# Attention and two MoE layers on one core: first-pass scores on 128 rows, scores cut at 512 columns, and constant matmuls in planned pauses

## Chip, cores and metric

One core of one Trainium2 chip. The metric is device time of one execution in microseconds (us), smaller is better; the time before is the median of three runs. Engines are named as the profile names them: PE (TensorE matmul), PEld (TensorE weight load), DVE (VectorE), ACT (ScalarE), POOL (GpSimd), SP (SyncE, which issues all DMAs here).

## What is computed

Batch 4, 8 heads, 576 positions, head size 64; then two MoE-like layers on 2304 tokens with 512 features and 2048 hidden units.

```
scores = q @ k.T / 8
attn   = exp(scores - max), kept only where scores >= max - tau, divided by its sum
x      = attn @ v                       # rearranged to [2304, 512]
x      = (h * clip(h + 3, 0, 6) / 6) @ w_out,     h = x @ w_in
out    = (h * sigmoid(1.702 * h)) @ w2_out,       h = x @ w2_in
```

## The kernel before

The kernel writes every operation into a list (`add`, line 300) with an engine, a cost in ns, a nominal time and its reads and writes. `Plan.settle` (line 220) runs a list scheduler over that list with those costs, and the operations are issued in the order of the planned starts (line 1075). So a cost written in the code sets the order in which instructions stand on each engine; it does not change how long they take.

Attention works in 16 units, a unit being a batch and a pair of heads (`unit`, line 486). A unit has nine score tiles of 128 queries by 576 keys. Each tile goes through the same chain: scores on PE into PSUM (`ps`, a ring of two places), row maximum on DVE (R, line 589), threshold (TH, line 590), exponential on ACT (X, line 591), mask and sum on DVE (M, line 592). Then `e` is transposed (line 643 and `blocks`) and multiplied with v (lines 684 and 701). The ring of two means that the scores of a tile can start only when M of the tile two before it is done.

Units 0 to 3 (batch 0, `early`) take the scores in plain fp32 (`score`, line 564) in two passes: pass 0 covers the first 256 queries of both heads, four tiles, each alone; pass 1 the rest, in pairs of heads. The two heads of a unit lie on rows 0 to 63 and 64 to 127 of one tile of q and one of k, and a single-head tile uses the 64 rows of its head. The trace shows an fp32 matmul as two records. Units 4 to 15 (`score2`, line 550) take them in fp32r: the keys are split in a high part `kh` and a low part `kl`, and a score tile is four matmuls, high and low times the two halves of the keys, 288 columns each (the fifth tile has eight). Each of them loads its 128 x 128 weights anew. I call four such matmuls a set.

Beside the attention of batch 0, 16 weight tiles of the first layer are decoded from 64-bit words (`decode`, line 376: ACT lines 347 and 400, DVE lines 401 to 403, POOL line 350) and split (`split`, line 407). The layer's matmuls (`gated`, line 750, line 760; `out_mm`, line 777, line 780) run between the score tiles of the next batch, in PSUM tiles `pm` of four banks.

`two` (line 368) is a constant of zeros and ones, set by three memsets on POOL. `g` is a ring of eight buffers for the hidden activations.

Of the kernel before, what the change touches and what calls it, by code (L numbers as in the profile page):

```python
# [9 lines left out]
F32 = mybir.dt.float32  # L10
F32R = mybir.dt.float32r
# [7 lines left out]
P = 128  # L19
# [41 lines left out]
class Plan:  # L61
# [158 lines left out]
    def settle(self):  # L220
# [9 lines left out]
            length = self.order(key)  # L230
        return sorted(self.ops, key=lambda o: (self.start[o.n], o.n))


def kicked(key, length, seed):

# [7 lines left out]
def tile_top_attention_moe_moe2(  # L243
# [19 lines left out]
    HF = NF // 2  # L263
    SH = S // 2
    CH = [(0, 256), (256, 320)]
    FULL = EXACT = 4
    scale = 0.125


# [58 lines left out]
    def f32(ap):  # L328
        return ap.bitcast(F32)

    def pe(n):
        return 7 + 0.43 * n
# [152 lines left out]

    def unit(u, b, j, t0):

        early, exact = u < FULL, u < EXACT
# [8 lines left out]
        def tile_():  # L497
            return buf("kqv", 12, "st", [P, QC], F32R)

        if exact:  # L500
            khb, qhb = tile_(), tile_()
        pieces = [(0, 0, 0, S)] + ([(1, 0, 0, 256), (1, 256, 320, 256), (1, 576, 256, 64)] if b == 0 else [(1, 0, 64, 512), (1, 576, 0, 64)])

        def of_head(x, hd):
            return [(x, ("z", hd))] + [(x, (h, o)) for h, o, _, _ in pieces if h == hd]

        def load_q(x, ap):
            for hd, z in ((0, 576), (1, 512)):
                add(POOL, 100, K("ld"), "qz", lambda hd=hd, z=z: nc.gpsimd.memset(ap()[64 * hd:64 * hd + 64, z:z + 64], 0.0), [], [(x, ("z", hd))])
            for hd, o, i, n in pieces:  # L510
                move(K("ld"), "ldq", 256 * n, lambda hd=hd, o=o, i=i, n=n: nc.sync.dma_start(out=ap()[64 * hd:64 * hd + 64, o:o + n], in_=q2[b, 2 * j + hd, :64, i:i + n]), [], [(x, (hd, o))])

        def load_k(x, ap):
            for hd in range(2):
                move(K("ld"), "ldk", 256 * S, lambda hd=hd: nc.sync.dma_start(out=ap()[64 * hd:64 * hd + 64, :S], in_=k2[b, 2 * j + hd, :64]), [], [(x, hd)])

        if exact:
            load_q(qhb, lambda: f32(qhb.t))
            load_k(khb, lambda: f32(khb.t))
            for rows, hds in ((slice(0, 64), (0,)), (slice(64, P), (1,))) if u == 0 else ((slice(0, P), (0, 1)),):  # L520
                add(DVE, 69 + 0.521 * QC, K("qs"), "qs", lambda rows=rows: nc.vector.tensor_scalar(out=f32(qhb.t)[rows], in0=f32(qhb.t)[rows], scalar1=sc_b.t[rows], scalar2=1.0, op0=ALU.mult, op1=ALU.mult),
                    [sc_b], [x for hd in hds for x in of_head(qhb, hd)])
# [26 lines left out]

        def score2(s):  # L550

            ps, t = buf("ps", 2, "ps", [P, 2, 512]), tiles[s]

            def mm(hd, q0, st, sp):
                for w, a, z in ((khs, st, False), (kls, False, sp)):
                    for i in range(2):
                        nc.tensor.matmul(ps.t[:, i, :SH], qss[hd].t[:, q0:q0 + P], w[hd].t[:, i * SH:(i + 1) * SH], start=a, stop=z)  # L557

            for hd in range(2) if t is None else t[:1]:
                q0 = t[1] * P + 128 * hd if t else 0 if hd else 512  # L560
                add(PE, 4 * pe(SH), K("S", s), "S", lambda hd=hd, q0=q0: mm(hd, q0, t is not None or hd == 0, t is not None or hd == 1), [qss[hd], khs[hd], kls[hd]], [ps])
            soft(s, ps)

        def score(ss):

            pss = {s: buf("ps", 2, "ps", [P, 2, 512]) for s in ss}

            def mm():
                for i in range(2):
                    for s in ss:  # L570
                        t = tiles[s]
                        rows, q0 = (slice(0, P), 512) if t is None else (slice(64 * t[0], 64 * t[0] + 64), t[1] * P)
                        nc.tensor.matmul(pss[s].t[:, i, :SH], f32(qhb.t)[rows, q0:q0 + P], f32(khb.t)[rows, i * SH:(i + 1) * SH], start=True, stop=True)  # L573

            add(PE, 4 * 243 + 300 + 40 * (len(ss) > 1), K("S", ss[0]), "S", mm, [qhb, khb] if len(ss) > 1 or tiles[ss[0]] is None else of_head(qhb, tiles[ss[0]][0]) + [(khb, tiles[ss[0]][0])], [pss[s] for s in ss])
            for s in ss:
                soft(s, pss[s])

        def soft(s, ps):

            t = tiles[s]
            e = buf("er", 1, "e", [P, S]) if t is None else buf("e", 5, "e", [P, S])
            e_of[s] = e
            c = slice(col[s], col[s] + 1)

            def ev():
                return e.t.rearrange("p (j s) -> p j s", j=2)

            add(DVE, 665, K("R", s), "R", lambda: nc.vector.tensor_reduce(out=nm.t[:, c], in_=ps.t[:, :, :SH], op=ALU.max, axis=AX.XY, negate=True), [ps], [(nm, s)])  # L589
            add(DVE, 121, K("TH", s), "TH", lambda: nc.vector.tensor_scalar(out=th.t[:, c], in0=nm.t[:, c], scalar1=-1.0, scalar2=nt_b.t, op0=ALU.mult, op1=ALU.add), [(nm, s), nt_b], [(th, s)])  # L590
            add(ACT, 624, K("X", s), "X", lambda: nc.scalar.activation(out=ev(), in_=ps.t[:, :, :SH], func=ACTF.Exp, bias=nm.t[:, c]), [ps, (nm, s)], [e])  # L591
            add(DVE, 729, K("M", s), "M", lambda: nc.vector.scalar_tensor_tensor(out=ev(), in0=ps.t[:, :, :SH], scalar=th.t[:, c], in1=ev(), op0=ALU.is_ge, op1=ALU.mult, accum_out=sm.t[:, c]),  # L592
                [ps, (th, s)], [e, (sm, s)])

        def recip(ss, s):
# [472 lines left out]
    for half in range(2):  # L1068
# [3 lines left out]
        if half == 0:  # L1072
            w = [fetch_pair(HF + f, kept[f // 2], t - 30000 + 4800 * f) for f in range(0, HF, 2)]

    order = pl.settle()
    with tc.manual_schedule():
        for op in order:
            op.fn()


# [49 lines left out]
```

## Time and profile before

| | |
|---|---|
| median of 3 runs | 1101.16 us (1094.9 to 1102.49) |
| profiled execution | 1101.79 us, its span 1100.0 us |
| PE busy | 1061.1 us, 96% of the span, 7400 matmul records |
| DVE, ACT, POOL busy | 725.8, 632.6, 512.3 us |
| mean granted PE clock by the profile | 0.993 of 2.4 GHz |

A busy time is the union of an engine's records, and matmul records overlap, so a busy PE need not stream all the time. The clock column repeats what the profiler recorded of the grant.

### The profile page before, as it was taken

What the parts mean: (1) busy time and instruction counts of PE and PEld (TensorE: products, weight loads), DVE (VectorE), ACT (ScalarE), POOL (GpSimd) and SP (SyncE); (2) the same over time, 40 slices, a digit from 0 to 9 for tenths busy, and PEclk for the clock granted to TensorE, in tenths of its full rate; (3) what the DMA queues carried; (4) which work ended last, traced back from release to release, by engine and by line L of the source; (5) the groups of instructions that cost most, each with busy time, mean ns of one, the idle gap of its engine ahead of it and who ended that gap; (6) DMA issues with size and microseconds to landing.
All of it is one profiled execution on the core that took longest, in us unless ns stands there. A gap on an engine that the chain in (4) does not pass through costs nothing.

```text
span 1100.0 us, 20256 instructions
## 1 busy us (share of the span) xinstructions
PE 1061.1 (96%) x7400; PEld 957.0 (87%) x7400; DVE 725.8 (66%) x1535; ACT 632.6 (58%) x1272; POOL 512.3 (47%) x592
## 2 busy tenths in 40 slices
PE   7988989989999999999999999999999999999998
PEld 4666878879988999899999999988988888889888
DVE  5898877677676766467876333678787674663634
ACT  3778766566666665576555324565656565444533
POOL 1578867777687775555376224451313322001100
PEclk9999989999999999999999999999999999999999
DMA  6234265556365635445754211335635443312202
GB/s 202 91 99 133 90 201 145 163 155 171 116 183 154 167 98 140 139 131 163 208 177 144 70 57 60 124 112 160 194 130 177 158 141 104 115 40 77 92 1 72
DMA packets 86852, 141.77 MB, mean 129 GB/s; under 512 B 8544, under 2 KB 50656, under 8 KB 85216
## 3 DMA queue, kind: packets, MB, share of 16 engines
q1 hardware_dynamic: 86752, 140.48, 41.9%
q8 instruction: 58, 0.95, 0.3%
q14 instruction: 42, 0.34, 0.1%
HBM read 97.32 MB, written 43.12 MB: 128 GB/s over the span
## 4 chain that ended last, share of the span: by engine, by line
PE 74%; DVE 9%; DMA 6%; ACT 5%; POOL 3%; issue 2%; SPq 0%; POOLq 0%; ACTq 0%; DVEq 0%
PE py L780 22%; PE pm L760 15%; PE pm L917 13%; PE pm L780 8%; PE pm L701 5%; PE pm L643 4%; PE ps L557 4%; PE ps L573 2%; DMA qk<-in_k_dram 2%; DVE outlring L350 2%; DVE g L350 1%; DVE tc L350 1%; ACT e L591 1%; POOL kqv L350 1%; DVE e L592 1%
## 5 line engine op out<-in xcount | busy, mean ns | idle before, releaser
L780 PE MATMUL py<-g,outhring 128*128 128x512 f32 (+2 forms) x1152 | 288.2, 337 | 3.9 <-DVE g L350 2.9
L780 PEld LDWEIGHTS py<-g,outhring 128*128 128x128 f32 x1152 | 193.8, 188 | 24.0 <-DVE g L350 6.9
L780 PE MATMUL py<-g,outlring 128*128 128x512 f32 (+2 forms) x576 | 193.4, 336 | 0.0
L760 PE MATMUL pm<-xh,inhring 128*128 128x256 f32 (+1 forms) x512 | 153.6, 300 | 0.0
L760 PE MATMUL pm<-xl,inhring 128*128 128x256 f32 (+1 forms) x512 | 151.6, 296 | 0.7 <-POOL xl L350 0.7
L760 PE MATMUL pm<-xh,inlring 128*128 128x256 f32 (+1 forms) x512 | 151.2, 295 | 0.0
L917 PE MATMUL pm<-outhring,inhring 128*128 128x256 f32 x512 | 144.8, 283 | 3.6 <-ACT u L347 2.6
L917 PE MATMUL pm<-outlring,inhring 128*128 128x256 f32 x512 | 143.9, 281 | 0.4 <-DVE outlring L350 0.4
L917 PE MATMUL pm<-outhring,inlring 128*128 128x256 f32 x512 | 143.6, 280 | 0.0
L589 DVE TENSOR_REDUCE nm<-ps 128x1 f32<-128x576 f32 x144 | 106.7, 751 | 50.1 <-PE ps L557 37.3
L350 POOL TENSOR_TENSOR g<-t,g 128x256 fp32r<-128x256 f32 (+1 forms) x104 | 87.8, 848 | 80.3 <-ACT g L347 77.3
L592 DVE SCALAR_TENSOR_TENSOR e<-ps,th,e 128x576 f32<-128x576 f32 x128 | 102.5, 809 | 29.0 <-ACT e L591 27.6
L780 PEld LDWEIGHTS py<-g,outlring 128*128 128x128 f32 x576 | 108.2, 188 | 10.0
L591 ACT ACTIVATE e<-ps,nm 128x576 f32<-128x576 f32 x128 | 93.2, 737 | 37.0 <-DVE nm L589 34.7
L772 DVE SCALAR_TENSOR_TENSOR t<-t,pm 128x256 f32<-128x256 f32 (+1 forms) x128 | 57.5, 449 | 85.9 <-ACT t L771 85.4
L350 POOL TENSOR_TENSOR wmstg<-wmstg,wrstg 128x512 uint32<-128x512 uint32 x48 | 64.7, 1349 | 94.7 <-DVE wmstg L403 74.6
L350 POOL TENSOR_TENSOR g<-tc,g 128x512 fp32r<-128x512 f32 x24 | 31.8, 1326 | 164.9 <-ACT g L347 133.9
L780 PE MATMUL pm<-g,outhring 128*128 128x256 f32 (+1 forms) x512 | 107.2, 300 | 0.8 <-POOL g L350 0.8
L771 ACT ACTIVATE t<-pm,half 128x256 f32<-128x256 f32 (+1 forms) x128 | 63.7, 498 | 75.4 <-PE pm L760 68.5
L917 PEld LDWEIGHTS pm<-outhring,inhring 128*128 128x128 f32 x512 | 96.9, 189 | 7.6 <-ACT u L347 3.0
L917 PEld LDWEIGHTS pm<-outlring,inhring 128*128 128x128 f32 x512 | 96.9, 189 | 3.1 <-DVE outlring L350 0.6
L760 PEld LDWEIGHTS pm<-xh,inhring 128*128 128x128 f32 x512 | 97.1, 190 | 1.2 <-issue 0.9
(108 smaller groups left out, 2410.0 us busy)
## 6 DMA issues: line engine op xcount, KB each, us to landing
turned<-tr SPq DMA_DIRECT2D x12, 1024.0 KB, 4.0
et<-turned SPq DMA_DIRECT2D x48, 256.0 KB, 5.8
wrawstg<-in_w1i_dram SPq DMA_DIRECT2D x16, 512.0 KB, 3.8
wrawstg<-in_w1o_dram SPq DMA_DIRECT2D x16, 512.0 KB, 3.7
wrawstg<-in_w2i_dram SPq DMA_DIRECT2D x16, 512.0 KB, 3.9
wrawstg<-in_w2o_dram SPq DMA_DIRECT2D x16, 512.0 KB, 4.0
qk<-in_k_dram SPq DMA_DIRECT2D x24, 288.0 KB, 3.3
qk<-in_q_dram SPq DMA_DIRECT2D x24, 288.0 KB, 3.5
```

The lines of the kernel that those rows point to most:

```text
L350: return lambda: (nc.vector if eng == DVE else nc.gpsimd).tensor_tensor(out=o(), in0=a(), in1=b(), op=op)
L557: nc.tensor.matmul(ps.t[:, i, :SH], qss[hd].t[:, q0:q0 + P], w[hd].t[:, i * SH:(i + 1) * SH], start=a, stop=z)
L589: add(DVE, 665, K("R", s), "R", lambda: nc.vector.tensor_reduce(out=nm.t[:, c], in_=ps.t[:, :, :SH], op=ALU.max, axis=AX.XY, negate=True), ...
L591: add(ACT, 624, K("X", s), "X", lambda: nc.scalar.activation(out=ev(), in_=ps.t[:, :, :SH], func=ACTF.Exp, bias=nm.t[:, c]), [ps, (nm, s)] ...
L592: add(DVE, 729, K("M", s), "M", lambda: nc.vector.scalar_tensor_tensor(out=ev(), in0=ps.t[:, :, :SH], scalar=th.t[:, c], in1=ev(), op0=ALU ...
L643: nc.tensor.transpose(pt.t[:kn, o:o + P], e_of[s].t[:, keys(k)], id_b.t)
L701: nc.tensor.matmul(pv[p].t[64 * hd:64 * hd + 64, :CH[p][1]], v_(k, hd), x, start=k == 0, stop=k == 4)
L760: nc.tensor.matmul(ph.t[:, :n], a, v, start=(cc == 0 and i == 0), stop=(cc == KC - 1 and i == 2))
L771: add(ACT, 93 + act(n), K("RL"), "RL", lambda: nc.scalar.activation(out=tt_(), in_=pt(), func=ACTF.Relu, scale=1.0 / 6.0, bias=half_b.t), ...
L772: add(DVE, dve(n), K("GT"), "GT", lambda: nc.vector.scalar_tensor_tensor(out=tt_(), in0=tt_(), scalar=1.0, in1=pt(), op0=ALU.min, op1=ALU. ...
L780: nc.tensor.matmul(py.t[:, :n], a, v, start=(st and i == 0), stop=(sp and i == 2))
L917: nc.tensor.matmul(o.t[:, :n], u.t[:, ws], v.t[:, xv], start=(st and kk == 0 and i == 0), stop=(sp and kk == 1 and i == 2), skip_group_che ...
```

## The change

Four things are changed.

1. Pass 0 of units 0 to 3 uses a new `score1`. Its queries lie in a buffer of their own, `qzb` (taken from the ring `g`): 256 columns per head, with zeros on the 64 rows of the other head. So the matmul runs over all 128 rows of k, and the other head's rows are multiplied by zero. q is loaded in two steps, the part for pass 0 first. The zeros are POOL memsets (64 x 256 twice and 64 x 64 twice a unit), and the scaling of q by 1/8 on DVE is cut in two, 512 and 384 columns.
2. A score place `ps` is [128, 1024] where it was [128, 2, 512]. `score1` and `score2` cut the 576 keys into 512 and 64 columns where `score2` had 288 and 288, and R, X and M read 576 columns in one row. Pass 1 of units 0 to 3 keeps the halves of 288.
3. The plan's order is run through `fill`: wherever the planned end of one PE operation and the planned start of the next leave room, matmuls of `two` by itself (128 x 128, fp32, line 1108) are issued into a `pm` bank that the plan has free there; nobody reads their result. Before 12 us of planned time it is one for each 450 ns, later one for each 216 ns after the first 300. In all, 94 of them.
4. `two` is set on DVE, ahead of everything else there.

```diff
+    def fill(self, order, make):
...
+                count = int((s - t) / 450 if s < 12000 else (s - t - 300) / 216)
...
-        add(POOL, 100, -30000, "two", lambda rows=rows, cols=cols, v=v: nc.gpsimd.memset(two_b.t[cols if rows == 64 else slice(0, P), cols], v), [], [two_b])
+        add(DVE, 100, -40000, "two", lambda rows=rows, cols=cols, v=v: nc.vector.memset(two_b.t[cols if rows == 64 else slice(0, P), cols], v), [], [two_b])
...
-            ps, t = buf("ps", 2, "ps", [P, 2, 512]), tiles[s]
+            ps, t = buf("ps", 2, "ps", [P, 1024]), tiles[s]
 
             def mm(hd, q0, st, sp):
                 for w, a, z in ((khs, st, False), (kls, False, sp)):
-                    for i in range(2):
-                        nc.tensor.matmul(ps.t[:, i, :SH], qss[hd].t[:, q0:q0 + P], w[hd].t[:, i * SH:(i + 1) * SH], start=a, stop=z)
...
+                    for c0, c1 in ((0, 512), (512, S)):
+                        nc.tensor.matmul(ps.t[:, c0:c1], qss[hd].t[:, q0:q0 + P], w[hd].t[:, c0:c1], start=a, stop=z)
...
+        def score1(s):
+
+            ps, (hd, m) = buf("ps", 2, "ps", [P, 1024]), tiles[s]
+            q0 = 256 * hd + m * P
+
+            def mm():
+                for c0, c1 in ((0, 512), (512, S)):
+                    nc.tensor.matmul(ps.t[:, c0:c1], f32(qzb.t)[:, q0:q0 + P], f32(khb.t)[:, c0:c1], start=True, stop=True)
...
+    def busy(i, count):
+
+        def run():
+            t = pools["pm"].tile([P, 512], F32, tag=f"pm{i}", name="pm")
+            for _ in range(count):
+                nc.tensor.matmul(t[:, :P], two_b.t, two_b.t, start=True, stop=True)
+
+        return run
```

How the order moves is shown at three places. The first is PE at the start of the program, before:

```order
L573 MATMUL ps<-kqv 128x288 x10
L643 MATMUL pm<-id,e 128x128 x8
L573 MATMUL ps<-kqv 128x288 x2
L643 MATMUL pm<-id,e 64x128 x4
L573 MATMUL ps<-kqv 128x288 x2
```

and with the change (L582 is `score1`, `g` the ring that `qzb` is taken from):

```order
L1108 MATMUL pm<-two 128x128 x10
L582 MATMUL ps<-kqv,g 128x512
L582 MATMUL ps<-kqv,g 128x64
L582 MATMUL ps<-kqv,g 128x512
L582 MATMUL ps<-kqv,g 128x64
L1108 MATMUL pm<-two 128x128 x4
```

Ten constant matmuls stand ahead of the first two score tiles and four behind them; eight and five follow within the next five tiles.

The second is the DMA queue of SP at the start, before:

```order
L362 DMA tau<-in_tau_dram 128x1
L511 DMA kqv<-in_q_dram 64x576
L515 DMA kqv<-in_k_dram 64x576
L511 DMA kqv<-in_q_dram 64x256 x2
L511 DMA kqv<-in_q_dram 64x64
```

and with the change:

```order
L381 DMA tau<-in_tau_dram 128x1
L525 DMA g<-in_q_dram 64x256 x2
L526 DMA kqv<-in_k_dram 64x576 x2
L525 DMA g<-in_q_dram 64x256 x2
L526 DMA kqv<-in_k_dram 64x576 x2
```

The first score tile stands behind q and k of one head before, behind q and k of both heads now; the first raw weight tile comes in the queue's 17th place where it was in the 27th.

The third is PE in the attention of units 4 to 15, behind the multiplication with v of the third of them. Before (L701 is that multiplication, L557 `score2`):

```order
L701 MATMUL pm<-et,kqv 64x256 x10
L701 MATMUL pm<-et,kqv 64x320 x10
L557 MATMUL ps<-kqv 128x288 x12
L643 MATMUL pm<-id,e 64x128 x4
L780 MATMUL pm<-g,outhring_1411 128x320 x2
```

and with the change (L729 was L701, L566 was L557, L671 was L643; three tiles of scores stand where the dots are):

```order
L729 MATMUL pm<-et,kqv 64x256 x10
L729 MATMUL pm<-et,kqv 64x320 x10
...
L671 MATMUL pm<-id,e 64x128 x4
L1108 MATMUL pm<-two 128x128 x7
L566 MATMUL ps<-kqv 128x512
L566 MATMUL ps<-kqv 128x64
L566 MATMUL ps<-kqv 128x512
L566 MATMUL ps<-kqv 128x64
```

A score tile is 512 and 64 columns twice, and seven constant matmuls stand where matmuls of the first layer stood; 26 stand between this multiplication and the next.

## Rows read from the trace of the kernel before

**Rows 1.** The page, its heads.

```profile
span 1100.0 us, 20256 instructions
PE 1061.1 (96%) x7400; PEld 957.0 (87%) x7400; DVE 725.8 (66%) x1535; ACT 632.6 (58%) x1272; POOL 512.3 (47%) x592
```

**Rows 2.** Windows: length, busy us by engine, granted clock, DMA share, GB/s.

```profile
core 0: us, PE busy (x) PEld busy (x) DVE busy (x) ACT busy (x) POOL busy (x), PEclk, DMA share, GB/s
10.00:20.00 10.00, 8.32 (x23) 5.38 (x23) 7.18 (x17) 3.94 (x6) 0.55 (x2) 1.00 0.62 172
20.00:30.00 10.00, 10.00 (x29) 6.06 (x28) 6.48 (x18) 5.97 (x11) 1.84 (x3) 1.00 0.80 285
30.00:40.00 10.00, 9.79 (x53) 6.50 (x53) 7.14 (x18) 6.59 (x12) 5.92 (x7) 1.00 0.34 107
40.00:60.00 20.00, 19.23 (x125) 12.94 (x124) 19.29 (x46) 16.30 (x31) 13.14 (x16) 1.00 0.29 91
68.20:71.60 3.40, 3.40 (x13) 2.74 (x13) 2.34 (x7) 0.77 (x2) 2.11 (x4) 0.50 0.67 245
110.00:143.00 33.00, 30.32 (x230) 25.55 (x230) 29.45 (x70) 24.27 (x47) 29.62 (x37) 1.00 0.36 119
143.30:150.10 6.80, 5.75 (x27) 5.60 (x28) 2.80 (x9) 3.52 (x6) 5.03 (x8) 0.50 0.97 264
174.10:177.40 3.30, 3.30 (x16) 3.26 (x15) 1.48 (x4) 3.15 (x7) 1.30 (x3) 0.50 0.05 17
```

**Rows 3.** The chain that ended last, 0 to 160 us: start, length, what.

```profile
1.16 0.56 SPq L511
1.76 3.01 DMA kqv<-in_k_dram
4.90 2.27 PE ps L573 x4
...
29.79 1.90 PE pm L643 x8
31.69 3.50 PE pm L684 x20
35.19 1.16 PE ps L573 x4
...
52.86 0.87 PE pm L643 x8
```

**Rows 4.** Timeline of PE near 375 us: start, length, what.

```profile
375.20 0.70 PE L557 MATMUL ps<-kqv 128*128 128x288 f32 x4
375.73 0.28 PE L780 MATMUL pm<-g,outhring 128*128 128x256 f32 x1
```

**Rows 5.** Timeline of PE near 833 us, matmuls of 512 columns.

```profile
832.81 0.40 PE L780 MATMUL py<-g,outlring 128*128 128x512 f32 x1
833.04 0.39 PE L780 MATMUL py<-g,outhring 128*128 128x512 f32 x1
```

**Rows 6.** Timeline of PEld at 345.5 us, weight loads behind a wait.

```profile
345.50 0.19 PEld L760 LDWEIGHTS pm<-xl,inhring 128*128 128x128 f32 x1 [0.54 <-POOL xl L350]
345.61 0.19 PEld L760 LDWEIGHTS pm<-xh,inlring 128*128 128x128 f32 x1
345.73 0.19 PEld L760 LDWEIGHTS pm<-xh,inhring 128*128 128x128 f32 x1
```

**Rows 7.** Groups of instructions by form, the scores of units 4 to 15.

```profile
L557 PE MATMUL ps<-kqv 128*128 128x288 f32 x480 | 83.0, 303 | 1.8 <-DVE e L592 1.2 <-DVE th L590 0.6
```

**Rows 8.** Windows over units 4 to 15, columns as in rows 2.

```profile
118.00:250.00 132.00, 122.84 (x897) 107.93 (x896) 98.39 (x244) 84.89 (x165) 98.61 (x136) 0.96 0.53 154
250.00:325.00 75.00, 74.91 (x573) 67.02 (x573) 51.68 (x130) 47.25 (x94) 53.33 (x72) 1.00 0.52 149
325.00:350.00 25.00, 22.94 (x174) 19.58 (x173) 16.65 (x42) 14.71 (x30) 17.34 (x25) 1.00 0.55 142
350.00:435.00 85.00, 84.96 (x658) 77.45 (x657) 61.37 (x155) 54.18 (x109) 56.45 (x81) 1.00 0.47 139
```

**Rows 9.** The same for line 557 alone: PE busy, PEld busy.

```profile
250.00:325.00 75.00, 18.31 (x108) 15.33 (x108) 1.00 0.52 149
350.00:435.00 85.00, 22.37 (x132) 18.70 (x132) 1.00 0.47 139
```

**Rows 10.** The chain that ended last, 138 to 180 us.

```profile
165.57 6.49 DMA qk<-in_k_dram
```

More of the change, by code (lines that the diff above doesn't have):

```diff
@@ L231, in settle @@
         return sorted(self.ops, key=lambda o: (self.start[o.n], o.n))
+    def fill(self, order, make):
+        used = [[] for _ in range(BANKS)]
+        for b in self.banks:
+            ops = [x[0] for x in b.access]
+            used[b.bank].append((min(self.start[o.n] for o in ops), max(self.start[o.n] + o.cost for o in ops) + 250))
+        out, end = [], 0.0
+        for op in order:
+            if op.eng == PE:
+                t, s = end, self.start[op.n]
+                end = max(end, s + op.cost)
+                count = int((s - t) / 450 if s < 12000 else (s - t - 300) / 216)
+                if count > 0:
+                    slack = max((min([t - y for _, y in u if y <= t] + [1e9]), -i) for i, u in enumerate(used) if not any(x < s and y > t for x, y in u)) if any(not any(x < s and y > t for x, y in u) for u in used) else None
+                    if slack is not None:
+                        out.append(make(-slack[1], count))
+            out.append(op.fn)
+        return out
 def kicked(key, length, seed):
@@ L486, in unit @@
     def unit(u, b, j, t0):
-        early, exact = u < FULL, u < EXACT
+        early = u < FULL
         tiles = [(0, 0), (1, 0), (0, 1), (1, 1), None, (0, 2), (1, 2), (0, 3), (1, 3)]
@@ L498, in tile_ @@
             return buf("kqv", 12, "st", [P, QC], F32R)
[L500 to L511, printed above, removed]
@@ L513, in load_k @@
-        def load_k(x, ap):
-            for hd in range(2):
[L515 to L522, printed above, removed]
+        if early:
+            khb, qhb, qzb = tile_(), tile_(), buf("g", HF, "gp", [P, 640], F32R)
+            for hd in range(2):
+                r, o = slice(64 * hd, 64 * hd + 64), slice(64 - 64 * hd, P - 64 * hd)
+                add(POOL, 260, K("ld"), "qz", lambda o=o, c=256 * hd: nc.gpsimd.memset(f32(qzb.t)[o, c:c + 256], 0.0), [], [(qzb, ("z", hd))])
+                add(POOL, 100, K("ld"), "qz", lambda o=o, c=256 + 64 * hd: nc.gpsimd.memset(f32(qhb.t)[o, c:c + 64], 0.0), [], [(qhb, ("z", hd))])
+                move(K("ld"), "ldq", 256 * 256, lambda r=r, c=256 * hd, h=2 * j + hd: nc.sync.dma_start(out=f32(qzb.t)[r, c:c + 256], in_=q2[b, h, :64, :256]), [], [(qzb, (hd, 0))])
+                move(K("ld"), "ldk", 256 * S, lambda r=r, h=2 * j + hd: nc.sync.dma_start(out=f32(khb.t)[r, :S], in_=k2[b, h, :64]), [], [(khb, hd)])
+            add(DVE, 69 + 0.521 * 512, K("qs"), "qs", lambda: nc.vector.tensor_scalar(out=f32(qzb.t)[:, :512], in0=f32(qzb.t)[:, :512], scalar1=sc_b.t, scalar2=1.0, op0=ALU.mult, op1=ALU.mult),
+                [sc_b], [(qzb, x) for hd in range(2) for x in (("z", hd), (hd, 0))])
+            for hd, o, i, n in ((0, 0, 256, 320), (1, 320, 256, 64), (1, 0, 320, 256)):
+                move(K("ld") + 4000, "ldq", 256 * n, lambda hd=hd, o=o, i=i, n=n: nc.sync.dma_start(out=f32(qhb.t)[64 * hd:64 * hd + 64, o:o + n], in_=q2[b, 2 * j + hd, :64, i:i + n]), [], [(qhb, (hd, o))])
+            add(DVE, 69 + 0.521 * 384, K("qs") + 4000, "qs", lambda: nc.vector.tensor_scalar(out=f32(qhb.t)[:, :384], in0=f32(qhb.t)[:, :384], scalar1=sc_b.t, scalar2=1.0, op0=ALU.mult, op1=ALU.mult), [sc_b], [qhb])
@@ L571, in mm, with soft @@
                         t = tiles[s]
-                        rows, q0 = (slice(0, P), 512) if t is None else (slice(64 * t[0], 64 * t[0] + 64), t[1] * P)
-                        nc.tensor.matmul(pss[s].t[:, i, :SH], f32(qhb.t)[rows, q0:q0 + P], f32(khb.t)[rows, i * SH:(i + 1) * SH], start=True, stop=True)
-            add(PE, 4 * 243 + 300 + 40 * (len(ss) > 1), K("S", ss[0]), "S", mm, [qhb, khb] if len(ss) > 1 or tiles[ss[0]] is None else of_head(qhb, tiles[ss[0]][0]) + [(khb, tiles[ss[0]][0])], [pss[s] for s in ss])
+                        rows, q0 = (slice(0, P), 256) if t is None else (slice(64 * t[0], 64 * t[0] + 64), t[1] * P - 256)
+                        nc.tensor.matmul(two(s)[:, i, :SH], f32(qhb.t)[rows, q0:q0 + P], f32(khb.t)[rows, i * SH:(i + 1) * SH], start=True, stop=True)
+            add(PE, 4 * 243 + 300 + 40 * (len(ss) > 1), K("S", ss[0]), "S", mm, [qhb, khb], [pss[s] for s in ss])
             for s in ss:
-                soft(s, pss[s])
-        def soft(s, ps):
+                soft(s, pss[s], lambda s=s: two(s, SH), lambda e: e.t.rearrange("p (j s) -> p j s", j=2))
+        def soft(s, ps, scores, like):
             t = tiles[s]
@@ L586, in ev @@
             def ev():
[L587 to L589 removed]
+                return like(e)
+            add(DVE, 665, K("R", s), "R", lambda: nc.vector.tensor_reduce(out=nm.t[:, c], in_=scores(), op=ALU.max, axis=AX.XY if len(scores().shape) == 3 else AX.X, negate=True), [ps], [(nm, s)])
             add(DVE, 121, K("TH", s), "TH", lambda: nc.vector.tensor_scalar(out=th.t[:, c], in0=nm.t[:, c], scalar1=-1.0, scalar2=nt_b.t, op0=ALU.mult, op1=ALU.add), [(nm, s), nt_b], [(th, s)])
[L591 to L592 removed]
+            add(ACT, 624, K("X", s), "X", lambda: nc.scalar.activation(out=ev(), in_=scores(), func=ACTF.Exp, bias=nm.t[:, c]), [ps, (nm, s)], [e])
+            add(DVE, 729, K("M", s), "M", lambda: nc.vector.scalar_tensor_tensor(out=ev(), in0=scores(), scalar=th.t[:, c], in1=ev(), op0=ALU.is_ge, op1=ALU.mult, accum_out=sm.t[:, c]),
                 [ps, (th, s)], [e, (sm, s)])
@@ L1073, in tile_top_attention_moe_moe2, with run @@
             w = [fetch_pair(HF + f, kept[f // 2], t - 30000 + 4800 * f) for f in range(0, HF, 2)]
+    def busy(i, count):
+        def run():
+            t = pools["pm"].tile([P, 512], F32, tag=f"pm{i}", name="pm")
+            for _ in range(count):
+                nc.tensor.matmul(t[:, :P], two_b.t, two_b.t, start=True, stop=True)
+        return run
     order = pl.settle()
     with tc.manual_schedule():
-        for op in order:
-            op.fn()
+        for fn in pl.fill(order, busy):
+            fn()
 def kernel(**inputs):
```

18 lines of the change are left out of this document (12 added, 6 removed).

## The prediction, made before the run

> **What bounds the kernel now.** I read the page's heads first: PE is busy in 1061 of 1100 us [rows 1], so what counts is where PE works for nothing and where it waits. Then the windows of the start. From 20 to 30 us PE has a record in all of the time, and DVE, which has the largest share of the softmax, in 6.48 of 10; from 40 to 60 us DVE is busy in 19.29 of 20 [rows 2]. So the first 35 us hang on PE, the next 25 on DVE.
>
> The chain of waits says why. Eight transposes take 1.90 us at 29.8 and 0.87 at 52.9; four score records take 2.27 us at 4.9 and 1.16 at 35.2 [rows 3]. That is a factor of two, 1.2 against 2.4 GHz, though the clock column says 1.00 from the start [rows 2]: before its first record the column tells nothing, and the durations decide. The clock rose between 31.7 us, where 20 matmuls with v begin, and 35.2 [rows 3]. Up to then PE had done scores on 64 rows and transposes, the last ten microseconds without a pause, and had stayed at the lower level. So it wasn't pauses alone that held it there. Later the lower level shows three times, at 68, 143 and 174 us [rows 2].
>
> The Trainium skill (TensorE: Matmul & The Clock Gate, Part 4: PE-mode transpose) says that transposes don't count as a busy PE for the clock. The trace agrees for transposes with 64-row scores between them: 10.00 of 10 us busy and half the clock. By that rule the constant matmuls and the 128-row scores would raise it early.
>
> In units 4 to 15 (118 to 435 us) PE is busy in 74.91 of 75 and in 84.96 of 85 us in two stretches, but in 122.84 of 132 and 22.94 of 25 in the others [rows 8]; there the chain runs over other things too, a 6.5 us load of k for one [rows 10].
>
> **The start.** Ten constant matmuls stand ahead of the first scores. They wait only for `two`, which DVE sets first. A transpose of 128 columns takes about 0.24 us at the lower level (1.90 / 8), and a constant fp32 matmul is two records of that size: 10 x 0.48 = 4.8 us, about the time that PE waits for q and k now (until 4.90). So I expect the clock up some microseconds after PE's start instead of at 34. PE's work up to 35 us then halves and DVE becomes the limit. DVE's idle time from 10 to 40 us is 30 - 7.18 - 6.48 - 7.14 = 9.2 us [rows 2]; at the share of 40 to 60 us (96%) 1.2 would be left, so at most 8.0 are to be had. Two things take from it. The first tile now waits for q and k of both heads, two issues later on SP at about 0.6 us each (0.56 for one [rows 3]): 1.2 us. And with two score places a tile's chain leaves DVE gaps while the tiles are few. I take a gain of 5 us, with bounds of 0 (the clock comes up no earlier, or the gain is lost to POOL, below) and 8. The raw weights are issued earlier too, so the decode can fill DVE's and POOL's idle time.
>
> The new memsets lie on POOL, which has 0.55 us of work from 10 to 20 [rows 2]; two scalings of q for one and the memsets of `two` lie on DVE while it waits for q. Cost nothing; without that cover under 1 us. The 128-row scores themselves stream as many columns: 512 and 64 against twice 288. No gain, no loss on PE, whose pace doesn't bound there once the clock is up.
>
> **Scores of units 4 to 15.** The large term. A set is four matmuls of 288 columns now. It takes 0.53 us, from 375.20 to the next matmul at 375.73 [rows 4]. There are 480 / 4 = 120 sets [rows 7]. With the change a set is 512, 64, 512, 64. One of 512 takes 0.23 us from start to start [rows 5]. None of 64 stands in fp32r in this trace, so I bound it. From below: by the slope between 288 (0.1325) and 512 (0.23) a column is 0.435 ns, and 64 come to 0.035; the set is then 0.53 as before, no loss. From above: each matmul loads its weights, and it can't start before they are in. Behind a wait, where the next load has nothing else to wait for, it starts 0.11 us after the one before (345.50 to 345.61; the third, held by a matmul of 256 columns, 0.12 later) [rows 6]. So a load takes 0.11 us, which 288 or 512 columns hide and 64 can't. As much as 0.13, a matmul of 288, is the upper bound, 0.72 a set. I take 0.11, since it is a row of the same kind of weights: 2 x 0.23 + 2 x 0.11 = 0.68, 0.15 us more a set, 120 x 0.15 = 18 us of PE.
>
> The Trainium skill (TensorE: Matmul & The Clock Gate, Back-to-back issue gap) gives matmuls of up to 64 columns about 60 cycles, by my estimate 0.025 us at the full clock; by that the loss would be none. The Trainium skill (same page, LDWEIGHTS) also gives 107 ns for 128 columns of weights, and with this the trace agrees: 0.11.
>
> How much shows in the time? In the two stretches where PE never rests there are 108 + 132 records [rows 9], 60 sets, 9 us, which show whole. The other 60 sets, another 9 us, lie where PE rests 9.2 of 132 and 2.1 of 25 us [rows 8] and the chain partly runs over POOL, ACT and loads. Some of these waits begin at PE's own scores and move with them. I take 3.5 of 9. Together 12.5 us, bounds 0 (the lower bound of a matmul) and 18 (all shows; 0.72 a set would give 17 at the same share).
>
> R, X and M read the same 576 elements in one row. Bounded by nothing in the trace; 0.05 us either way on 108 tiles is 5 us of DVE, which is busy 51.68 of 75 [rows 8] and hides it. I take nothing.
>
> **The pauses.** The 94 constant matmuls take 0.22 us each at full clock (2 x 0.87 / 8, [rows 3]), 20 us in all. 27 stand in the first eight tiles. Where a planned pause is a real one they cost nothing; where PE runs late they delay what follows. 26 stand in one stretch of unit 6, where the plan has moved the layer's matmuls away. I take 1 us, bounds 0 and 5. What they may give back: at the half clock PE was busy 3.40, 5.75 and 3.30 us [rows 2], 6.2 us more than needed. But few stand at those places in the new order, so I take 2 of it, bounds 0 and 5.
>
> **Sum.** From the profiled execution, 1101.8: - 5 - 2 + 12.5 + 1 = 1108.3. It lies 0.6 us over the median of the runs, which moves nothing: 1108 us, 0.6% slower. A measurement of this kernel can tell about 1%, 11 us, from no change.
>
> **Rivals.**
> *The weight load hides.* The 64 columns cost only their stream. For it: the load engine could be two loads ahead. Against: each load in rows 6 starts only when the one before is done, or when the matmul before starts. The time would be 1101.8 - 7 + 1 = 1096; with the gains at their upper ends (8 and 4) 1091 and less. Chance 0.13, of which 0.06 under 1090. (It is the Trainium skill's issue gap from TensorE: Matmul & The Clock Gate, cited above, taken alone.)
> *The loss shows whole.* Slower. The place is PE in units 4 to 7, the price the 5.5 us that I let the waits hide. For it: a wait for POOL or ACT behind a tile begins at that tile's scores, so it isn't slack. It decides if PE's rest from 118 to 250 us stays near 9 us: 1101.8 - 7 + 18 + 1 = 1114. Chance 0.2.
> *The start's gain is lost to POOL.* From 110 to 143 us POOL is busy 29.62 of 33 [rows 2]; if its queue sets the pace there and doesn't start earlier, the 5 us end there: 1113. Against: the first decodes come earlier in the order. Chance 0.15.
> *The gains outgrow the loss.* Start 8, clock 5, and only the 9 us of the busy stretches lost: 1101.8 - 13 + 9 + 1 = 1099. Chance 0.12, a third of it under 1090 with less lost.
>
> **Chances.** My case, 1102 to 1112, has 0.40. Faster by over 1% (under 1090): 0.06 + 0.04 = 0.1. Slower by over 1% (over 1112): 0.2 and most of 0.15, 0.32. Within 1%: 0.58. The range from 1093 to 1119 holds all cases but the ends of the first and the last, and of the second and third together (1119).
>
> **What would show it.** Right, if the eight transposes near the start take 0.87 us before 15 us, DVE's share from 10 to 40 us is over 85%, the 36th row maximum comes some 5 us earlier; if a 512 and a 64 of line 566 take 0.34 us together and PE has no rest from 250 to 435 us. Wrong, if 64 columns take under 0.06 us, if the clock still rises at 34, or if the windows of 118 to 250 us take up all of the 9 us.

## The result and the profile after

| | before | after |
|---|---|---|
| median | 1101.83 us (1094.9 to 1103.02, 4 runs) | 1113.52 us (1109.58 to 1116.95, 4 runs) |
| profiled execution, its span | 1101.79, 1100.0 us | 1116.95, 1115.2 us |

The ratio is 1.0117, with a 95% interval of 1.0087 to 1.0147: the change costs 11.7 us. The forecast was 1108 us with a range of 1093 to 1119. The time lies in the range, but 5.5 us over the forecast and just outside the likeliest case.

The heads of the page after, against [rows 1]:

```profile
span 1115.2 us, 20645 instructions
PE 1085.8 (97%) x7588; PEld 977.7 (88%) x7588; DVE 733.0 (66%) x1541; ACT 634.2 (57%) x1272; POOL 511.4 (46%) x597
```

PE has 24.7 us more of records and 188 more of them, which are the 94 constants at two records each. The timeline of PE at the start, after (start, length, then what; idle time before it in brackets):

```profile
1.38 4.11 PE L1108 MATMUL pm<-two 128*128 128x128 f32 x20 [1.38 <-DVE two L388]
6.00 2.35 PE L582 MATMUL ps<-kqv,g 128*128 128x512 f32 x8 [0.51 <-DMA kqv<-in_k_dram]
...
15.69 1.04 PE L671 MATMUL pm<-id,e 128*128 128x128 f32 x8
```

The first constants are PE's first work, and the scores wait for k 0.51 us longer. Eight transposes are back at the short time at 15.69 us; in [rows 3] they still took 1.90 at 29.79. So the clock is up from the first score tiles on. Windows after, columns as in [rows 2] and [rows 8]:

```profile
10.00:20.00 10.00, 8.44 (x49) 6.19 (x50) 8.22 (x23) 5.21 (x9) 1.76 (x3) 1.00 0.92 246
20.00:30.00 10.00, 8.57 (x55) 5.73 (x56) 6.81 (x18) 6.01 (x11) 2.92 (x4) 1.00 0.83 240
30.00:40.00 10.00, 8.79 (x52) 5.41 (x52) 9.95 (x22) 8.11 (x15) 6.34 (x9) 1.00 0.38 112
114.00:250.00 136.00, 128.48 (x891) 108.50 (x890) 95.72 (x234) 79.97 (x153) 90.77 (x127) 0.97 0.48 140
250.00:325.00 75.00, 75.00 (x555) 67.34 (x556) 51.02 (x126) 47.26 (x94) 52.34 (x74) 1.00 0.51 140
...
172.00:178.80 6.80, 6.11 (x27) 5.27 (x28) 1.90 (x5) 3.76 (x8) 2.77 (x5) 0.50 0.01 2
```

DVE has 24.98 of 30 us from 10 to 40, 83%, where [rows 2] had 20.80. The lower level shows once after the start, 6.8 us at 172, where [rows 2] had it at three places. From 114 to 250 us PE still rests 7.5 us, from 250 to 325 not at all, and in the 25 us behind that 0.9.

The scores of units 4 to 15 and the row maximum, groups by form (busy us, mean ns), after:

```profile
L617 DVE TENSOR_REDUCE nm<-ps 128x1 f32<-128x576 f32 x144 | 106.9, 753 | 43.3 <-PE ps L566 37.2 <-PE ps L601 3.4 <-PE ps L582 0.5
L566 PE MATMUL ps<-kqv 128*128 128x512 f32 x240 | 90.1, 456 | 1.6 <-DVE e L620 1.4 <-DVE th L618 0.2
L566 PE MATMUL ps<-kqv 128*128 128x64 f32 x240 | 46.2, 192 | 0.0
```

A record's length holds its wait for weights, so the pace is read from starts. The timeline of PE after, two sets:

```profile
381.33 1.56 PE L566 MATMUL ps<-kqv 128*128 128x512 f32 x8
382.73 0.48 PE L808 MATMUL pm<-g,outhring 128*128 128x256 f32 x2
```

Eight records in 1.40 us are 0.70 a set, where [rows 4] has 0.53. The first matmul behind a set waits for weights too, so such a pair of starts is rough to a few hundredths.

### The profile page after: what moved, and what is told of

Same layout as the page of the kernel before. It is cut to its first block, busy times and chain, and to the rows that moved or that the text cites. A ratio compares the mean times of both kernels' runs of the same rounds, so it can differ in the third digit from the quotient of the medians.

```text
span 1115.2 us, 20645 instructions
## 1 busy us (share of the span) xinstructions
PE 1085.8 (97%) x7588; PEld 977.7 (88%) x7588; DVE 733.0 (66%) x1541; ACT 634.2 (57%) x1272; POOL 511.4 (46%) x597
## 4 chain that ended last, share of the span: by engine, by line
PE 77%; DMA 7%; DVE 6%; ACT 4%; issue 2%; SPq 2%; POOL 1%; ACTq 0%; DVEq 0%; POOLq 0%
PE py L808 23%; PE pm L788 16%; PE pm L945 13%; PE pm L808 8%; PE ps L566 6%; PE pm L729 5%; PE pm L671 4%; DMA qk<-in_k_dram 3%; DVE outlring L369 1%; PE pm L712 1%; PE pm L1108 1%; DVE tc L369 1%; ACT et L674 1%; DVE g L369 1%; DMA kept<-wmstg 1%
## 5 line engine op out<-in xcount | busy, mean ns | idle before, releaser
L617 DVE TENSOR_REDUCE nm<-ps 128x1 f32<-128x576 f32 x144 | 106.9, 753 | 43.3 <-PE ps L566 37.2
L808 PE MATMUL pm<-g,outhring 128*128 128x256 f32 (+1 forms) x512 | 111.2, 308 | 0.2 <-ACT ys L366 0.2
```

What stands on the lines that cost most here:

```text
L808: nc.tensor.matmul(py.t[:, :n], a, v, start=(st and i == 0), stop=(sp and i == 2))
```

## Experiments

Twelve kernels were run. Several expectations speak of "the first mult with v of unit 4" and "the first of the second pass of unit 4"; the second is the first mult with v of unit 8, four units on. The stretch between the two is units 4 to 7. The names of e1 to e12 stand for the labels.

### The parts of the change

**e1, halves.** After, with the cut of `score2` taken back (R, X and M read the two halves again, which isn't shown here):

```diff
-                    for c0, c1 in ((0, 512), (512, S)):
-                        nc.tensor.matmul(ps.t[:, c0:c1], qss[hd].t[:, q0:q0 + P], w[hd].t[:, c0:c1], start=a, stop=z)
+                    for i in range(2):
+                        nc.tensor.matmul(ps.t[:, 512 * i:512 * i + SH], qss[hd].t[:, q0:q0 + P], w[hd].t[:, i * SH:(i + 1) * SH], start=a, stop=z)
```

> The changed kernel with the scores of units 4 to 15 in halves of 288 again, nothing else undone. Theory A (the cut at 512 and 64 costs 0.16 us a set, 120 sets, and nearly all of it shows): 1113.5 - 19 = 1094 us, between 1091 and 1097, faster than before by 0.4 to 0.9%. Rival B (only part of it shows, as the prediction had it, 12.5 us, and the constant matmuls in later pauses cost the rest): 1101. The start as in the changed kernel, its clock up at about 5 us.

Measured: 1103.90 us (10 runs), ratio 1.003 [1.0011, 1.0049]. That is 2.6 over before, so the cut is worth 9.1 of the 11.7, and what is left of the change isn't a gain but a loss. Neither theory had this: the time is 3 us over the slower of the two.

**e4, e6, e7: which part raises the clock.** e4 is e1 without any constant, e6 is e1 with 64-row scores in pass 0, e7 is both.

```diff
-                if count > 0:
+                if False:
...
+                r = slice(64 * hd, 64 * hd + 64)
...
-                    nc.tensor.matmul(ps.t[:, c0:c1], f32(qzb.t)[:, q0:q0 + P], f32(khb.t)[:, c0:c1], start=True, stop=True)
+                    nc.tensor.matmul(ps.t[:, c0:c1], f32(qzb.t)[r, q0:q0 + P], f32(khb.t)[r, c0:c1], start=True, stop=True)
```

> The run with halves of 288, without any of the 94 constant matmuls; the 128-row scores stay. Theory A (the constants raise the clock and give the 5 us of the start): 1099, eight transposes near the start take 1.9 us. Rival C (128-row scores raise the clock by themselves, the constants aren't needed): 1094 as with them, transposes at 1.0 us from the second tile group on.

> The run with halves of 288 and all constants, but pass 0 of units 0 to 3 multiplies the 64 rows of its head alone instead of 128 rows with zeros. Theory A: the constants hold the clock, 1094, with at most 1 us from the changes between 64 and 128 rows. Rival C (the rows count): the clock falls back between 10 and 30 us and the time goes to 1097 to 1100.

> The run with halves of 288, pass 0 on 64 rows, no constants: what is left of the change is the order and the split loads of q. Theory A and rival C alike: the clock rises only with the first multiplications with v, at 25 to 35 us, and the time is that of before, 1099 to 1102. If it is much less, the order and not the clock gave the gain.

Measured: e4 1103.56 (9 runs), 1.003 [1.0014, 1.0046]; e6 1104.49 (10), 1.0032 [1.0011, 1.0053]; e7 1106.80 (5), 1.0057 [1.0034, 1.0079]. All three lie 4 to 5 us over the slower of their forecasts, which gave the new order no price. The timeline of PE at the start of e7, and behind it that of e4:

```profile
18.25 1.97 PE L672 MATMUL pm<-id,e 128*128 128x128 f32 x8
...
35.24 1.09 PE L672 MATMUL pm<-id,e 128*128 128x128 f32 x8
```

```profile
19.55 1.91 PE L671 MATMUL pm<-id,e 128*128 128x128 f32 x8
...
23.22 1.04 PE L671 MATMUL pm<-id,e 128*64 128x128 f32 x8
```

With 64 rows and no constants the transposes are slow at 18 us and fast only at 35, as before. With 128 rows alone they are fast at 23.2. In e4 the recorded clock was up before, then 0.50 from 13 to 23 us. So in these two executions the padded rows raised the clock without the constants, though later, and by the medians they are worth 3.2 us (e7 to e4). With all the constants the rows make no difference that the intervals show (e1 and e6).

**e5, constants only at the start.** e1 with those planned before 12 us, 28 records or 14 constants; 80 later ones are left out. (The 27 and 67 of the expectation count by place: 27 stand in the first eight tiles, but 13 of them are planned later than 12 us.)

```diff
-                if count > 0:
+                if count > 0 and s < 12000:
```

> The changed kernel with halves of 288 and only the 27 constant matmuls of the start, without the 67 later ones. Theory D (the later ones stand in pauses that the run doesn't have, eight behind the last attention unit above all): 3 to 4 us faster than with them, 1100. Rival (they cost nothing, or keep the clock up for as much): 1104, unchanged.

Measured: 1100.13 (10 runs), 0.9999 [0.998, 1.0018]: no difference from before, as theory D had it. Each kernel taken against before on its own chip, the constants at the start give 3.6 us (e4 +2.3, e5 -1.3) and the later ones cost 3.9 (e1 +2.6). Both figures rest on e5. The intervals of e4 and e5 touch; e9 below, which is e5 but for the place of v's load, lies 3.2 over before; and e4 and e1, without any constants and with all, ran on one chip and are 0.3 us apart. One place looks like two of the 3.9 and isn't. The timeline of PE behind the last mult with v, e1 first, then e4:

```profile
443.03 5.07 PE L729 MATMUL pm<-et,kqv 128*64 128x256 f32 x40
448.04 2.05 PE L1108 MATMUL pm<-two 128*128 128x128 f32 x16
450.14 0.39 PE L788 MATMUL pm<-xh,inhring 128*128 128x256 f32 x1
```

```profile
442.12 5.07 PE L729 MATMUL pm<-et,kqv 128*64 128x256 f32 x40
447.12 0.39 PE L788 MATMUL pm<-xh,inhring 128*128 128x256 f32 x1
...
462.14 0.39 PE L808 MATMUL pm<-g,outhring 128*128 128x256 f32 x1 [0.78 <-POOL g L369]
```

Eight constants stand between the mult and the first layer where the plan had a pause and PE has none: 7.1 us from mult to layer where e4 has 5.0. But without them the layer then waits for POOL, 0.78 us in the last line, and with them it doesn't. The matmul of that line starts at 463.31 in e1, 1.2 us behind e4, and the mult was already 0.9 behind. So nearly all of the 2 us is made up within 20 us.

**e2, the cut alone.** Before, with `score2` cut at 512 on a flat reading of `ps`, which R, X and M also use; order untouched.

```diff
-                    for i in range(2):
-                        nc.tensor.matmul(ps.t[:, i, :SH], qss[hd].t[:, q0:q0 + P], w[hd].t[:, i * SH:(i + 1) * SH], start=a, stop=z)
+                    for c0, c1 in ((0, 512), (512, S)):
+                        nc.tensor.matmul(flat()[:, c0:c1], qss[hd].t[:, q0:q0 + P], w[hd].t[:, c0:c1], start=a, stop=z)
```

> The kernel before with the scores of units 4 to 15 cut at 512 and 64 and read in one row, nothing else of the change. Theory A2 (a set costs 0.16 us more, 19 us in all, and some two thirds of it show): 1101.3 + 10 to 13 = 1111 to 1114. If all shows: 1120. If the loss of the changed kernel comes from its new order: under 1105.

Measured: 1110.61 (4 runs), 1.008 [1.005, 1.011], 9.2 us over before, as much as the cut is worth from e1 to after. So the cut costs the same in either order, as far as the medians tell.

**e3, six matmuls a set.** Before, with 288, 160 and 128 columns instead of 288 and 288, high and low of a piece in turn.

```diff
+                for i, c0, c1 in ((0, 0, SH), (1, 0, 160), (1, 160, SH)):
...
+                        for w in (khs, kls):
+                            nc.tensor.matmul(ps.t[:, i, c0:c1], qss[hd].t[:, q0:q0 + P], w[hd].t[:, i * SH + c0:i * SH + c1],
```

> The kernel before with each set of four matmuls (288, 288 twice) as six (288, 160, 128 twice). Theory L (a matmul can't be shorter than its weight load, 0.11 us): a set takes 2 x 0.13 + 4 x 0.11 = 0.70 us, as with the cut at 512 and 64, and the time is that of the cut alone within 3 us. Rival P (fp32r matmuls of few columns take four times as long per column): 160 columns 0.27, 128 columns 0.21, a set 1.2 us, the time over 1140.

Measured: 1114.33 (4 runs), 1.012 [1.0105, 1.0136]. The timeline of PE in e3, two sets:

```profile
380.88 1.64 PE L561 MATMUL ps<-kqv 128*128 128x288 f32 x12
382.35 0.45 PE L783 MATMUL pm<-g,outhring 128*128 128x256 f32 x2
```

A set takes 1.47 / 2 = 0.735 us. Two of 288 are 0.265 of it [rows 4], so the four short ones take 0.12 each, as a matmul of 64 does in after, (0.70 - 2 x 0.23) / 2 = 0.12. For 160 and 128 columns the slope of the forecast, 0.435 ns a column, gives 0.07 and 0.06. In the trace's single records the loads beside the short ones start 0.11 us apart, one behind the other, as the loads behind the wait in [rows 6] do. So a short matmul costs the time of a weight load, whatever its columns: more small matmuls cost by their number. Rival P falls. The time is 3.7 us over e2's, a little more than theory L allowed.

### Where the gain of the start goes

e5 has the early clock and no cut, and no gain. A set of 14 constants in the old order tells whether the new order is to blame.

**e8, constants in the old order.** Before, its order untouched, with the 14 constants put where `fill` finds planned pauses before 12 us; the tile is one of ones, set by DVE.

```diff
+        nc.vector.memset(fil_b.t, 1.0)
+        for fn in pl.fill(order, busy):
+            fn()
```

> The kernel before, its order untouched, with 14 constant matmuls at the start of PE (of a tile of ones of their own). The clock should rise at about 6 us. Theory E (the new order, not the clock, loses the start's gain in units 4 to 7): the gain of some 4 us at the first tiles stays, 1097. Rival F (units 4 to 7 go at the pace of their loads, POOL and ACT in any order): the first multiplication of unit 4 comes 3 to 5 us earlier than 153.8, that of unit 8 no more than 1, and the time is 1100 to 1102.

Measured: 1099.84 (10 runs; 1095.48 to 1103.37), 0.999 [0.997, 1.001]. The time is what rival F said, the landmarks what theory E said. The first mult with v of unit 4 and of unit 8 on PE's timeline, in before, then e8, e1 and after:

```profile
153.75 3.46 PE L701 MATMUL pm<-et,kqv 128*64 128x256 f32 x28
...
257.89 5.07 PE L701 MATMUL pm<-et,kqv 128*64 128x256 f32 x40
```

```profile
149.25 5.07 PE L722 MATMUL pm<-et,kqv 128*64 128x256 f32 x40
...
253.68 5.07 PE L722 MATMUL pm<-et,kqv 128*64 128x256 f32 x40
```

```profile
147.38 5.07 PE L729 MATMUL pm<-et,kqv 128*64 128x256 f32 x40
...
256.50 5.07 PE L729 MATMUL pm<-et,kqv 128*64 128x256 f32 x40
```

```profile
148.34 5.07 PE L729 MATMUL pm<-et,kqv 128*64 128x256 f32 x40
...
261.99 3.19 PE L729 MATMUL pm<-et,kqv 128*64 128x256 f32 x26
```

At unit 4 after is 5.4 us ahead of before, e1 6.4 and e8 4.5. Units 4 to 7 take 104.1 us before and 104.4 in e8, but 109.1 in e1, and 107.8 and 108.1 in e7 and e4 by the same reading. e6 takes 108.1. (e5 takes 111.0, but its profiled run is its slowest and has the lower clock for 17 us of the stretch.) So 3.7 to 5.0 us are lost in units 4 to 7 in the new order, with and without constants, at either number of rows, each read from one execution. The old order keeps its gain to unit 8. By units, the largest part lies between the mults of units 4 and 5: 27.4 us before and 27.5 in e8, 29.5 to 30.4 in e1, e4, e6 and e7. The clock isn't the reason there: the lower level lasted 3.4 us in before, e8, e1, e4 and e6, and didn't show in e7.

The chain of waits shows loads of k in that stretch. Before (the first is [rows 10]), then e1:

```profile
193.95 6.11 DMA qk<-in_k_dram
221.24 5.62 DMA qk<-in_k_dram
```

```profile
160.96 7.39 DMA qk<-in_k_dram
192.15 7.19 DMA qk<-in_k_dram
217.34 6.54 DMA qk<-in_k_dram
```

They are about a microsecond longer each in e1. In its order the load of v is issued behind the four et<-turned DMAs and right ahead of that of k; in the old order it stands ahead of the four. That was the theory of the next two runs.

**e9 and e10, the place of v's load.** e9 is e5 with v's load ahead of the four again, in four units; e10 is e8 with it behind them, in five. Only SP's order changes. The edit is that of e9; that of e10 is its mirror.

```diff
+    for o in [x for x in order if x.name == "ldv" and x.eng == SP]:
+        i = order.index(o)
+        sp = [x for x in order[:i] if x.eng == SP][-6:]
+        d = [x for x in sp if x.name == "DM"][-4:]
+        if len(d) == 4 and all(order.index(x) < order.index(d[0]) for x in o.deps):
+            order.remove(o)
+            order.insert(order.index(d[0]), o)
```

> The kernel with halves and with only the constants planned in the first 12 us (e5), its order on TensorE, VectorE, ScalarE and GpSimd untouched; on SP's queue the load of v (L552) goes ahead of the four et<-turned DMAs that stood before it, in four units, as in the kernel before. It leaves nothing out. Theory A (what the new order loses in units 4 to 7 is the load of v put behind those four DMAs and next to the load of k): from the first mult with v of unit 4 to the first of the second pass of unit 4 (the stretch that is 104.1 us before and 104.5 in e8, 107.9 to 111.0 in the kernels with the new order) about 105 to 107 us, the time about 1097, 3 us below e5. Theory B (the loss is in the order of TensorE's own work, the loads only follow it): the stretch stays 108 to 111, the time within 1 us of e5, 1099 to 1101.

> The opposite edit, on the kernel before with constants at the start (e8): its order on the other engines untouched, the load of v (L564) goes behind the four et<-turned DMAs that stood after it, in five units, as in the new order. It leaves nothing out. Theory A (the place of the load of v is what the new order loses): the stretch of units 4 to 7 that is 104.5 us in e8 grows to about 107 to 108, the time to about 1103, 3 us over e8. Theory B (TensorE's own order is it): the stretch stays at 104 to 105 and the time within 1 us of e8, 1099 to 1101.

Measured: e9 1103.09 (12 runs), 1.0021 [1.0005, 1.0036]; e10 1101.11 (12), 1.0008 [0.9988, 1.0028]. In e9 the stretch is 108.6 us and the time rather higher than e5's: theory A falls for e9. In e10 the stretch grew to 106.9 in the profiled run, as A said, but its time doesn't stand apart from e8's. That run is e10's slowest, and the lower clock lasted 3.4 us longer there than in e8's, which can be up to 1.7 of the 2.5 us. So the place of v's load may cost something in the old order, and putting it back doesn't mend the new one.

**e11 and e12, other orders of the same work.** e5 with one line changed (line 34; the expectation says 47): the planner shakes its priorities by a seed and settles on another order. The "list of starts" in the expectations is the planner's own, from the costs in the code; no device time is in it.

```diff
-KICKS = ()
+KICKS = (13,)
```

> The same operations as e5 (halves, 128-row scores, only the constants planned in the first 12 us) in another order: the planner is given one seed to shake its priorities (KICKS = (13,), line 47) and settles on another order of the same work. It leaves nothing out. In the planner's own list of starts the first mult with v of unit 4 stands at 140.1 us and the last, of unit 15, at 423.3 for before; at 139.7 and 425.8 for the order that after, e1 and e4 to e7 share; at 135.4 and 421.5 for this one. Theory A (what units 4 to 7 lose is this one order of the planner's, not the work of the change): 4 us earlier at 421 and 423 than e5's order, so the time 1094 to 1097, faster than before. Theory B (the work of the change costs 4 us in units 4 to 7 in any order, or the list of starts says nothing of the chip): 1099 to 1103, as e5 and e9.

> As e11 with another seed (KICKS = (4,)). It leaves nothing out. In the planner's list the first mult with v of unit 4 stands at 139.4 us, the first of the second pass of unit 4, four units on, 100.4 later (before 99.6; the order of after, e1 and e4 to e7 102.5; e11 102.4), the last of unit 15 at 423.5. Theory A: the stretch from the first mult of unit 4 to that of the second pass, 107.9 to 111.0 on the chip in the new order and 104.1 before, is 105 to 106 here, and the time about 1098, 2 us below e5. Theory B: it stays 108 to 111 and the time 1099 to 1103.

Measured: e11 1092.91 (6 runs; 1091.84 to 1096.37), ratio 0.9948 [0.993, 0.9967]; e12 1095.21 (12 runs), 0.9962 [0.9945, 0.9978]. Both are faster than before, and the same operations in e5's order are not: over before, e5 has -1.3 us, e11 -7.0, e12 -4.7, each against before on its own chip. The two mults on PE's timeline, e11, then e12:

```profile
143.66 5.07 PE L729 MATMUL pm<-et,kqv 128*64 128x256 f32 x40
...
251.69 5.07 PE L729 MATMUL pm<-et,kqv 128*64 128x256 f32 x40
```

```profile
146.44 5.07 PE L729 MATMUL pm<-et,kqv 128*64 128x256 f32 x40 [1.67 <-DMA et<-turned]
...
252.12 5.07 PE L729 MATMUL pm<-et,kqv 128*64 128x256 f32 x40
```

e12 does what theory A says in units 4 to 7: 105.7 us. e11 takes 108.0 there, as its list of starts has it, but comes to unit 4 3.7 us ahead of e1. Either way unit 8 is reached at 252, 4.4 to 4.8 us ahead of e1 and 6 ahead of before. So the work that the change adds doesn't force the loss in units 4 to 7: e12 does the same work without it. The loss goes with the order, and e11 makes up for it ahead of unit 4. Which instructions in that order cost the time is open: the place of v's load was tried and isn't enough. Whether the work of before would also be faster in another order wasn't tried, so the 7 us of e11 are not all the change's.

## Why the prediction was right, and where it was not

The pieces are taken from the times over before, in us, each in its own comparison. They add up because each is the step from one row to the next:

| step | over before | piece |
|---|---|---|
| new order, split loads of q, pass 0 cut at 512, 64 rows, no constants (e7) | +5.5 | +5.5 |
| 128-row scores (e4) | +2.3 | -3.2 |
| constants at the start (e5) | -1.3 | -3.6 |
| later constants (e1) | +2.6 | +3.9 |
| cut at 512 (after) | +11.7 | +9.1 |

By the ratios in place of the medians the pieces are +6.3, -3.0, -3.4, +3.4 and +9.6. That of the cut is borne out by e2. Those of rows and constants hold for this sequence only: with all the constants in, the rows give 0.6 (e6 to e1), and with the rows in, all the constants together give nothing (e4 to e1).

**The cut** was the large term, and its mechanism held. By its starts a set takes 0.70 us where I had 0.68. e2 keeps the order of before, so the two can be laid side by side matmul by matmul: a set adds 0.15 us in the median, as I had, and 120 sets 18 us. Of these 9.1 show (9.2 in e2), where I had 12.5: 9 whole in the two stretches without rest and 3.5 elsewhere. In the profiled run of e2 the same matmul comes 2.1 us later than before at 250 us, 5.6 at 325 and at 350, and 10.2 at 435. So 8.1 of the 9 show in the two stretches, and 2.1 of the 3.5 elsewhere, though 60 sets stand there too: what failed is how much the waits hide. (My price for the upper bound was off: 0.72 a set is 0.19 more, which at the same share gives 16 and not 17.) The mults of units 8, 11 and 15 on PE's timeline in e2, then the last two in before, where that of unit 8 is at 257.89:

```profile
260.12 5.07 PE L704 MATMUL pm<-et,kqv 128*64 128x256 f32 x40
...
342.69 5.07 PE L704 MATMUL pm<-et,kqv 128*64 128x256 f32 x40
...
452.61 5.07 PE L704 MATMUL pm<-et,kqv 128*64 128x256 f32 x40
```

```profile
337.11 5.07 PE L701 MATMUL pm<-et,kqv 128*64 128x256 f32 x40
...
442.41 5.07 PE L701 MATMUL pm<-et,kqv 128*64 128x256 f32 x40
```

They are 2.2, 5.6 and 10.2 us apart. From e1 to after units 4 to 7 grow by 4.6 us, 109.1 to 113.7, in the profiled runs; but that of after is its slowest and has the lower clock for 6.8 us there where e1 has 3.4, so it isn't shown that less of the cut hides in the new order. The rival "the loss shows whole" came to 1114, near the result, by the wrong way. "The weight load hides" is out.

The Trainium skill (TensorE: Matmul & The Clock Gate, Back-to-back issue gap) gives a matmul of up to 64 columns about 60 cycles, by my estimate 0.025 us; it is a figure for a single matmul, and the page says itself that it leaves the weight load out. Measured here, with new weights for each, it was 0.12, so taken alone the figure doesn't price such a matmul. The load of 107 ns that the same page gives (LDWEIGHTS) is what it comes near.

**The start** came as told: the clock is up early, the transposes are short at 15.69 us (I said before 15), DVE has 83% from 10 to 40 us (I said over 85), the 36th row maximum comes 4.6 us earlier, and the first mult of unit 4 comes 5.4 us earlier (I said 5). The step that failed is the next one, which I didn't write down: that a lead at unit 4 stays a lead to the end. I counted what the new order moved at three places and took it to cost nothing else. It loses 3.7 to 5.0 us in units 4 to 7 (e1, e4, e6, e7), and what the start gives in the end (e5) is 1.3 us, which the interval doesn't tell from nothing.

"The start's gain is lost to POOL" told the size, 1113, but not the place or the cause. POOL isn't later: it has 90.77 us from 114 to 250, 67%, where [rows 8] has 75%, and the lead is still there at the first mult of unit 4.

**The pauses** were undersized: 1 us in the sum, 3.9 measured, by e5 alone. It lies within my bound of 5. I had named the stretch with 26 constants, and there no loss shows: from the mult of unit 6 to that of unit 8 it is 52.7 us in e1 and 52.4 in e6, and 52.4 to 53.0 in e4, e5 and e7 without them. From the mult of unit 8 to that of unit 15 it is 186.5 and 186.1 against 184.5, 184.5 and 184.3. So about 2 us of the loss can be placed, and the rest stays open.

**The clock's low stretches**: I took 2 us for them. The lower level showed once in after, 6.8 us, where it had shown three times, 13.5 us [rows 2]. No run takes this alone. But the later constants did keep the clock up in the profiled runs. Windows of e4, without them, and of e1, with them, columns as in [rows 2]:

```profile
205.00:232.00 27.00, 21.61 (x146) 15.74 (x146) 18.69 (x46) 14.77 (x28) 16.14 (x23) 0.87 0.51 141
205.00:232.00 27.00, 25.11 (x192) 19.24 (x189) 17.53 (x45) 14.17 (x27) 16.46 (x24) 1.00 0.52 141
```

This is where the 26 stand. The clock is 0.81 to 0.87 in e4, e5, e7 and e9, which lack them, and 1.00 in after, e1 and e6, and the time from unit 6 to unit 8 is the same with and without, as said under the pauses. It looks as if the constants took as much of PE as the clock gave back, so nothing of my 2 us shows there; in the order of before the clock stays at 1.00 there without them.

**R, X and M** read one row of 576 as fast as two halves: the group of the row maximum in before, against 753 ns in after:

```profile
L589 DVE TENSOR_REDUCE nm<-ps 128x1 f32<-128x576 f32 x144 | 106.7, 751 | 50.1 <-PE ps L557 37.3 <-PE ps L573 12.3
```

Nothing, as told.

**The sum.** From +6.5 to +11.7: start and clock, with the price of the new order in it, gave -1.3 in place of -7, which adds 5.7 (e11 wins 5.7 back by another order alone); the cut 9.1 in place of 12.5 takes 3.4 off; the pauses 3.9 in place of 1 add 2.9. That the forecast came within 5.5 us is in part luck: the cut's error has the opposite sign.

## What to carry to other kernels

Where a planner makes the order, a change of costs or reads makes another order, and this can cost as much as the change gains: compare the planner's own starts at a few landmarks for both (here it had the last mult with v 2.5 us later), and try some other orders of the new work before judging it; one seed turned a kernel equal to before into one 0.5% faster. Among the three orders of the same work the planner's place for the last mult, 421.5, 423.5 and 425.8 us, ranked them as the chip did, but before, at 423.3, was slower than e12. Cut matmuls that load their own weights so that none is shorter than its load. All 94 constants together gave nothing here: those at the start seem to pay where PE truly waits, the later ones to cost about as much, even where they keep the clock up.

## What the runs showed that was not expected

The same program for PE at the start raised the clock in one execution and not in another. e8 and e10 differ only on SP, from 155 us on. PE's timeline in the profiled run of e8, then of e10:

```profile
1.03 3.78 PE L1101 MATMUL pm<-fil 128*128 128x128 f32 x16 [1.03 <-DVE fil L1107]
4.75 1.56 PE L594 MATMUL ps<-kqv 64*128 64x288 f32 x4
...
8.97 1.23 PE L594 MATMUL ps<-kqv 64*128 64x288 f32 x4
```

```profile
1.03 3.78 PE L1101 MATMUL pm<-fil 128*128 128x128 f32 x16 [1.03 <-DVE fil L1114]
4.87 2.25 PE L594 MATMUL ps<-kqv 64*128 64x288 f32 x4
...
25.62 1.97 PE L664 MATMUL pm<-id,e 128*128 128x128 f32 x8
```

Eight constants take the same 3.78 us; then four score records take 1.56 and soon 1.23 in e8, and 2.25 in e10, where the transposes are still slow at 25.6 us. So constants there don't hold the clock up for certain. This can be why e8, whose profiled run led by 3.7 us, has a median gain of 1.6 that its interval doesn't tell from none, and why its times spread over 8 us; only these two starts of the program were seen, so it isn't shown. In the seven other traced kernels with constants at the start (after, e1, e5, e6, e9, e11, e12) the first clock record, at the full level, comes at 4.4 to 7.6 us.

Scores over all 128 rows, half of them zeros, were followed by the higher clock at 23 us in e4, where the same scores on 64 rows, with transposes between them as there, had the lower one until 33 in e7. PE had records in more of the time in e7, 7.54 and 9.37 us of 10 from 10 and from 20 us on, than in e4, 6.34 and 8.77. After e8 and e10, one execution of each isn't proof; that the medians lie 3.2 us apart speaks for it.
